# Attention and a maxout expert layer on one core: the probabilities of query blocks 0 and 1 transposed together, and a new order around them

## The chip, the core and the metric

The kernel runs on one NeuronCore of a Trainium2 chip. The metric is the device time of one execution in microseconds (us). The core has five engines with an instruction queue each: TensorE (PE in the profile; its weight loads are shown as PEld), VectorE (DVE), ScalarE (ACT), GpSimd (POOL) and SyncE (SP). SP computes nothing here: it issues nearly all DMAs. Each engine runs its own queue in order and waits on semaphores for the others. TensorE's clock is granted at one of two levels, 1.2 or 2.4 GHz; the profile shows it as a share, 0.50 or 1.00.

## What is computed

```python
# q, k, v: (8, 8, 576, 64) float32; s: (8, 8, 576) float32
scores = q @ k.T / sqrt(64)                        # per batch and head
cum  = cumsum(maximum(s, 0), axis=-1)
bias = -(cum[..., :, None] - cum[..., None, :])
scores = where(causal, -1e9, scores + minimum(bias, 0))
attn = softmax(scores) @ v                         # (8, 8, 576, 64)
x = attn as (4608, 512)                            # heads side by side
h = maximum(maximum(x @ w1, x @ w2), x @ w3)       # (4608, 768)
out = h @ w_out                                    # (4608, 512)
```

## The kernel before

A *visit* is one pair of heads of one batch item. Its 576 queries are five blocks of 128 (the last has 64), and one *step* is one query block of one visit. There are 160 steps and 40 visits. For batch items 0 and 1 a visit is cut in two: blocks 0 and 1 in visits 0 to 7, blocks 2, 3 and 4 in visits 8 to 15. Visits 16 to 39 (items 2 to 7) are *stacked* and have all five blocks. Visits 0 to 3 run in plain float32 and transpose on TensorE; all others keep each number as a sum of two float16 halves, high and low.

In a step, TensorE makes the scores (`scores`, two steps ahead), VectorE their row maximum (`highest`), ScalarE the exponentials (`expo`), and then `probs` divides: ScalarE writes the high halves (tile `prh`), VectorE the low halves (`prl`). SP transposes both by DMA into `ph` and `pl`. One step after the last block of a phase (phase 0: blocks 0 and 1; phase 1: blocks 2 to 4) `values` multiplies the transposed probabilities by `vh` and `vl`, the halves of v, into the PSUM tile `av`. So `values` of blocks 0 and 1 stands at the end of the step after block 1, and that of blocks 2 to 4 at the end of the next visit's block 0. `prh` and `prl` have two buffers each, taken in turn; `ph` and `pl` have one per phase.

When the four visits of an item and phase are done, `add_set` queues 22 expert groups: 18 of 12 matmuls (`pm`, with `x` and the weights `w`) and 4 of 18 (`po`, with `hh` and `hl`). They fill TensorE between the attention's own matmuls. The table `GROUPS` says for each step how many of them run ahead of the next scores and how many at the end of the step. What is left, 43 groups, runs after the last visit.

Loads and preparations stand in lists by step (`at`); the table `moved` shifts single ones by whole steps. For stacked visits these are `load_nat` (a load of 576 KB into `fixed`), the scaling and splitting of q and k (`nat_hi`, `nat_lo`, `nat_own` on GpSimd), and `nat_far`: four DMA copies on SP into the score operands `h` and `l`. `pair_scale2` and `bias_power` put the small matmuls `gmq` and `gmc` on TensorE. `hold` places dummy matmuls on `identb` (table `KEEP`).

In `probs`, for blocks 0 to 3, two transposes leave SP in each step:

```python
for c in range(2):
    nc.sync.dma_start_transpose(
        out=pT[c][:, 0:2 * m, i:i + P], in_=halves[c][:, 0:2 * m, :].rearrange("p n c -> p (n c)")
    )
```

Here m is the number of key blocks (block index + 1), and each has two heads, so block 0 transposes 2 tiles of 128 x 128 for each half, block 1 four, block 2 six and block 3 eight. Block 4 has four issues.

Of the kernel before, what the change touches and what calls it, by code (L numbers as in the profile page):

```python
# [21 lines left out]
"moved": ({('later_keys',): 1, ('load', 10): 1, ('load', 15): 1, ('load', 4): -3, ('load', 5): -3, ('load', 6): -5, ('load', 7):  # L22
-5, ('load_v', 10): 1, ('load_v', 11): -1, ('load_v', 19): -1, ('load_v', 20): 1, ('load_v', 21): 1, ('load_v', 24):
1, ('load_v', 25): 1, ('load_v', 26): 1, ('load_v', 28): 1, ('load_v', 29): 1, ('load_v', 30): 1, ('load_v', 32): 1,
('load_v', 33): 1, ('load_v', 34): 1, ('load_v', 37): 1, ('load_v', 4): -1, ('load_v', 5): -2, ('load_v', 6): -1,
('load_v', 7): -1, ('nat_bias', 18, 1): -1, ('nat_bias', 22, 0): 1, ('nat_bias', 23, 0): -1, ('nat_bias', 26, 0): 1,
('nat_bias', 27, 0): -1, ('nat_bias', 30, 0): 1, ('nat_bias', 34, 0): 2, ('nat_bias', 35, 0): -1, ('nat_bias', 38, 0):
1, ('nat_bias', 39, 0): -1, ('nat_hi', 16, 0): -1, ('nat_hi', 21, 0): -1, ('nat_hi', 21, 1): 1, ('nat_hi', 22, 0): -1,
('nat_hi', 25, 0): -1, ('nat_hi', 26, 0): -1, ('nat_hi', 26, 1): 1, ('nat_hi', 30, 0): -1, ('nat_hi', 30, 1): 1,
('nat_hi', 34, 0): -1, ('nat_hi', 34, 1): 1, ('nat_hi', 37, 0): -1, ('nat_hi', 38, 0): -1, ('nat_hi', 38, 1): 1,  # L30
('nat_own', 21, 0, 0): 2, ('nat_own', 21, 0, 1): 1, ('nat_own', 21, 1, 0): 1, ('nat_own', 21, 1, 1): 1, ('nat_own',
22, 0, 0): 1, ('nat_own', 22, 0, 1): 1, ('nat_own', 22, 1, 0): 1, ('nat_own', 22, 1, 1): 1, ('nat_own', 25, 0, 0): 1,
('nat_own', 25, 0, 1): 1, ('nat_own', 25, 1, 0): 2, ('nat_own', 25, 1, 1): 1, ('nat_own', 26, 0, 0): 1, ('nat_own',
26, 0, 1): 1, ('nat_own', 26, 1, 0): 2, ('nat_own', 26, 1, 1): 1, ('nat_own', 29, 0, 0): 1, ('nat_own', 29, 0, 1): 1,
('nat_own', 29, 1, 0): 1, ('nat_own', 29, 1, 1): 2, ('nat_own', 30, 0, 0): 1, ('nat_own', 30, 0, 1): 1, ('nat_own',
30, 1, 0): 1, ('nat_own', 30, 1, 1): 1, ('nat_own', 33, 0, 0): 1, ('nat_own', 33, 0, 1): 1, ('nat_own', 33, 1, 0): 1,
('nat_own', 33, 1, 1): 1, ('nat_own', 34, 0, 0): 2, ('nat_own', 34, 0, 1): 1, ('nat_own', 34, 1, 0): 1, ('nat_own',
34, 1, 1): 1, ('nat_own', 37, 0, 0): 1, ('nat_own', 37, 0, 1): 1, ('nat_own', 37, 1, 0): 1, ('nat_own', 37, 1, 1): 1,
('nat_own', 38, 0, 0): 1, ('nat_own', 38, 0, 1): 1, ('nat_own', 38, 1, 0): 1, ('nat_own', 38, 1, 1): 1, ('pair_max',
20, 0): 1, ('pair_max', 20, 1): 1, ('pair_max', 21, 0): 1, ('pair_max', 22, 1): 2, ('pair_max', 23, 0): 1,  # L40
('pair_max', 23, 1): 1, ('pair_max', 24, 0): 1, ('pair_max', 24, 1): 1, ('pair_max', 25, 0): 1, ('pair_max', 26, 0):
1, ('pair_max', 26, 1): 1, ('pair_max', 27, 0): 2, ('pair_max', 28, 0): 1, ('pair_max', 28, 1): 1, ('pair_max', 29,
0): 2, ('pair_max', 29, 1): 1, ('pair_max', 30, 0): 1, ('pair_max', 30, 1): 3, ('pair_max', 31, 0): 2, ('pair_max',
31, 1): 1, ('pair_max', 32, 0): 1, ('pair_max', 33, 0): 1, ('pair_max', 33, 1): 1, ('pair_max', 34, 0): 1,
('pair_max', 34, 1): 2, ('pair_max', 35, 0): 2, ('pair_max', 35, 1): 1, ('pair_max', 36, 0): 1, ('pair_max', 36, 1):
1, ('pair_max', 37, 0): 1, ('pair_max', 37, 1): 1, ('pair_max', 38, 0): 1, ('pair_max', 38, 1): 2, ('pair_max', 39,
0): 2, ('pair_max', 39, 1): 1, ('pair_scale3', 3): 1, ('prep2', 10): 1, ('prep2', 9): -1, ('prep3', 5): -1, ('prep3',
7): 1, ('prep3', 8): -1, ('prep5', 11): 1, ('prep5', 15): -1, ('prep5', 17): -1, ('prep5', 18): -1, ('prep5', 4): -1,
('prep5', 5): 1, ('prep5', 7): -1, ('vmax', 17): 1, ('vmax', 20): 1, ('vmax', 21): 2, ('vmax', 22): 1, ('vmax', 24):
1, ('vmax', 25): 1, ('vmax', 26): 1, ('vmax', 28): 1, ('vmax', 29): 1, ('vmax', 30): 1, ('vmax', 32): 1, ('vmax', 33):  # L50
2, ('vmax', 34): 1, ('vmax', 36): 1, ('vmax', 37): 1, ('vmax', 38): 1, ('nat_bias', 36, 1): -1, ('load_nat', 34): 1,
('decode4', 10): 1, ('prep5', 35): -1, ('prep3', 15): 2, ('nat_own', 32, 1, 0): 1, ('nat_far', 29, 0, 1): -1,
('nat_far', 38, 0, 0): 1, ('prep5', 6): -1, ('load_nat', 25): -2, ('nat_own', 24, 1, 1): 1, ('nat_bias', 37, 1): -1,
('nat_far', 23, 1, 1): -1, ('nat_far', 39, 0, 1): 1, ('nat_far', 25, 0, 1): -1, ('nat_own', 39, 0, 1): 1, ('nat_far',
36, 0, 0): -1, ('nat_far', 24, 0, 1): -1, ('nat_far', 18, 1, 0): 1, ('load_nat', 31): 1, ('prep4', 11): 1,
('load_nat', 26): -1, ('nat_far', 38, 1, 0): 1, ('load_nat', 28): -1, ('prep2', 6): 1, ('nat_hi', 24, 0): 1,
('nat_own', 36, 1, 0): 1, ('load_nat', 21): -1, ('prep2', 0): -1, ('decode4', 21): 1, ('nat_bias', 36, 0): -1,
('decode3', 3): -1, ('pair_max', 18, 1): 1, ('gram1', 0, 2): 1, ('prep4', 22): -1, ('decode3', 17): -1, ('load_nat',
27): 1, ('prep5', 13): 1, ('nat_bias', 25, 1): 1, ('load_w', 22): 1, ('nat_far', 28, 0, 0): 1, ('prep2', 3): 1,
('prep2', 11): 1, ('vmax', 39): 1, ('nat_own', 20, 0, 1): 1, ('nat_bias', 22, 1): 1, ('load_v', 31): 1, ('load_nat',  # L60
36): -1, ('nat_bias', 35, 1): -1, ('nat_own', 19, 1, 0): 1}),
# [1449 lines left out]
```

## Time and profile before

| what | value |
|---|---|
| median of 3 runs | 856.54 us (855.1 to 862.59) |
| profiled execution, its own time | 858.63 us |
| its span in the profile | 856.80 us |
| TensorE busy | 810.3 us, 95% |
| VectorE busy | 642.8 us, 75% |
| ScalarE busy | 533.6 us, 62% |
| GpSimd busy | 295.6 us, 35% |
| DMA queue of SP | 237,792 packets, 117 MB |

The busy times overlap, since the engines run side by side. The span is what the profile sees; the execution's own time is 1.83 us longer. Waits are named by the engine that ended them.

### The profile page before, as it was taken

How to read it: one execution, taken by the hardware profiler on the slowest of the kernel's cores; microseconds unless marked ns; L12 is line 12 of the kernel's file. 1: busy time of each engine (PE TensorE's matmuls, PEld its weight loads, DVE VectorE, ACT ScalarE, POOL GpSimd, SP SyncE). 2: the span in 40 equal slices, each digit the busy share in tenths (PEclk: the TensorE clock that was granted, in tenths of full speed). 3: DMA queues.
4: the chain of work that ended last, by engine and by line, in shares of the span. 5: the costliest groups of instructions: out<-in, count | busy, mean ns of one | idle time of the engine just before them, and what ended most of it. 6: DMA issues, size and time to landing. Idle time of an engine off the chain costs nothing.

```text
...
## 1 busy us (share of the span) xinstructions
PE 810.3 (95%) x6933; PEld 618.6 (72%) x6933; DVE 642.8 (75%) x1562; ACT 533.6 (62%) x1458; POOL 295.6 (35%) x532
## 2 busy tenths in 40 slices
...
GB/s 350 369 87 82 123 165 156 189 165 141 142 149 152 118 180 146 146 139 153 145 157 162 134 146 136 155 148 135 179 155 127 125 114 122 99 77 70 17 10 31
DMA packets 238464, 119.81 MB, mean 140 GB/s; under 512 B 210592, under 2 KB 219296, under 8 KB 238368
## 3 DMA queue, kind: packets, MB, share of 16 engines
q1 hardware_dynamic: 237792, 117.01, 63.1%
q10 hardware_dynamic: 576, 1.57, 0.6%
...
## 4 chain that ended last, share of the span: by engine, by line
PE 65%; DVE 16%; DMA 10%; ACT 5%; issue 3%; SPq 1%; POOL 1%; DVEq 0%; ACTq 0%
PE pm L1089 37%; PE po L1131 13%; PE av L957 6%; PE s L631 4%; DVE prl L812 3%; DMA pl<-prl 3%; DMA r<-in_w_dram 2%; DMA ph<-prh 2%; DVE w L1062 2%; DMA st<-in_start_dram 2%; ACT e L766 1%; DVE fixed L228 1%; DVE m L1106 1%; PE s L643 1%; ACT prh L809 1%
## 5 line engine op out<-in xcount | busy, mean ns | idle before, releaser
L1089 PE MATMUL pm<-x,w 128*128 128x320 f16 (+1 forms) x3240 | 424.4, 287 | 1.7 <-DVE m L1106 1.7
L1089 PEld LDWEIGHTS <-w 128*128 128x128 f16 x3240 | 311.8, 98 | 92.6 <-issue 5.8
L1095 POOL CAST hh<-m 128x320 f16<-128x320 f32 (+1 forms) x90 | 45.9, 511 | 348.7 <-DVE m L1106 256.3
L809 ACT ACTIVATE prh<-e,ri 128x128 f16<-128x128 f32 (+3 forms) x200 | 96.8, 529 | 100.5 <-DVE ri L793 90.1
L1106 DVE SCALAR_TENSOR_TENSOR m<-pm,m 128x320 f32<-128x320 f32 (+1 forms) x180 | 81.9, 455 | 91.4 <-PE pm L1089 73.8
L1131 PE MATMUL po<-hh,w 128*128 128x320 f16 (+1 forms) x720 | 141.5, 287 | 1.2 <-ACT kh L333 0.5
L812 DVE SCALAR_TENSOR_TENSOR prl<-e,ri,prh 128x128 f16<-128x128 f32 (+3 forms) x200 | 117.3, 624 | 21.6 <-ACT prh L809 12.8
L1131 PEld LDWEIGHTS <-w 128*128 128x128 f16 x1080 | 103.6, 98 | 33.0 <-issue 4.8
L735 DVE CUSTOM_DVE_ANT_0 s<-s,later,qf 128x128 f32<-128x128 f32 (+1 forms) x192 | 103.8, 551 | 16.8 <-PE s L631 13.7
L766 ACT ACTIVATE e<-s,nm 128x128 f32<-128x128 f32 (+4 forms) x216 | 105.5, 496 | 4.3 <-DVE nm L735 2.0
L1131 PE MATMUL po<-hl,w 128*128 128x320 f16 (+1 forms) x360 | 103.2, 287 | 1.3 <-POOL hl L1096 1.3
L253 POOL COPY h<-fixed 64x576 f16<-64x576 f16 x96 | 72.7, 779 | 56.2 <-DVE fixed L228 54.4
L1103 ACT ACTIVATE m<-pm 128x320 f32<-128x320 f32 (+1 forms) x90 | 36.5, 405 | 74.0 <-PE pm L1089 67.6
L809 ACT ACTIVATE prh<-s,ri 128x512 f16<-128x512 f32 x72 | 46.8, 684 | 41.6 <-DVE ri L793 36.2
L1096 POOL TENSOR_TENSOR hl<-m,hh 128x320 f16<-128x320 f32 (+1 forms) x90 | 69.9, 777 | 7.4
L957 PEld LDWEIGHTS <-vh 128*64 128x64 f16 x800 | 45.8, 110 | 30.1 <-issue 20.9
L1139 ACT ACTIVATE o<-po,os 128x320 f32<-128x320 f32 (+1 forms) x60 | 30.0, 499 | 49.5 <-PE po L1131 43.8
L812 DVE SCALAR_TENSOR_TENSOR prl<-s,ri,prh 128x512 f16<-128x512 f32 x72 | 51.8, 747 | 11.0 <-ACT prl L809 9.9
L957 PE MATMUL av<-ph,vh 128*64 128x320 f16 (+3 forms) x368 | 49.1, 282 | 7.5 <-DMA ph<-prh 7.5
L766 ACT ACTIVATE s<-s,nm 128x512 f32<-128x512 f32 (+1 forms) x72 | 48.5, 673 | 0.1
L631 PE MATMUL s<-h 128*128 128x128 f16 (+1 forms) x192 | 42.3, 299 | 3.4 <-DMA h<-fixed 2.2
L957 PE MATMUL av<-ph,vl 128*64 128x320 f16 (+3 forms) x368 | 44.0, 276 | 0.1
...
## 6 DMA issues: line engine op xcount, KB each, us to landing
...
```

What stands on the lines that cost most here:

```text
L253: nc.gpsimd.tensor_copy(out=R[v]["h"][own, j, x], in_=staged(v)[own, 3 - x])
L631: nc.tensor.matmul(ps[:, j, :nk], lhsT=w[:, c, qs], rhs=w[:, 1 - c, 0:nk], start=(x == "h" and not (lone and j)), stop=(x == "l"), skip_gr ...
L735: nc.vector.tensor_tensor_reduce(out=sc[:, j], in0=sc[:, j], in1=future[0][:, Q4 - nk:Q4], scale=n, scalar=3.0e38, op0=ALU.add, op1=ALU.mi ...
L766: nc.scalar.activation(out=to, in_=sc, func=AF.Exp, bias=nm[:, j:j + 1], scale=-1.0 if below(t) else 1.0, accum_out=sm[:, j:j + 1],)
L809: nc.scalar.activation(out=hi, in_=src, func=AF.Copy, scale=sc)
L812: nc.vector.scalar_tensor_tensor(out=lo, in0=src, scalar=sc, in1=hi, op0=ALU.mult, op1=ALU.subtract)
L957: nc.tensor.matmul(av[j * D:(j + 1) * D, c0:nq], lhsT=lt, rhs=rt, start=(n < 2), stop=(n >= len(todo) - 2), skip_group_check=True,)
L1089: nc.tensor.matmul(pm[:, :nq], lhsT=w[:, wt, kt, :], rhs=xt, start=(n == 0), stop=(n == 3 * NKT - 1))
L1095: nc.gpsimd.tensor_copy(out=st["hh"][:, ft, :nq], in_=m1[:, :nq])
L1096: nc.gpsimd.tensor_tensor(out=st["hl"][:, ft, :nq], in0=m1[:, :nq], in1=st["hh"][:, ft, :nq], op=ALU.subtract)
L1106: nc.vector.scalar_tensor_tensor(out=m1[:, :nq], in0=pm[:, :nq], scalar=HSC, in1=m1[:, :nq], op0=ALU.mult, op1=ALU.max)
L1131: nc.tensor.matmul(pm[:, :nq], lhsT=W[18 + ft][:, wt, dt, :], rhs=st[ht][:, ft, :nq], start=(n == 0), stop=(n == 3 * NFT - 1),)
```

## The change

For blocks 0 and 1 on the float16 path (28 visits: 4 to 7 and 16 to 39), block 0 takes a pair of tiles `prh`, `prl` and writes its two 128 x 128 pieces into places 0 and 1, and issues nothing. Block 1 takes the same pair, writes its four pieces into places 2 to 5, and one issue for each half transposes all six. The transposed tile is [128, 6, 128] instead of [128, 4, 256], and `values` reads the columns of key block 0 from two places of it, in a pattern of two runs of 128. The numbers of matmuls and their columns stay.

```diff
         ph = 0 if qb < 2 else 1
         if qb in (0, 2):
             PT[v, ph] = [
-                att.tile([P, 4 + (4 + 2 * n) * ph, PH[ph][1]], F16, tag=f"pT{c}{ph}", name=f"p{c}{t}", bufs=1)
+                att.tile([P, 4 + (4 + 2 * n) * ph, PH[ph][1]] if ph else [P, 6, P], F16, tag=f"pT{c}{ph}", name=f"p{c}{t}", bufs=1)
...
-        halves = [att.tile([P, 8, P], F16, tag=f"pr{c}", name=f"pr{c}{t}") for c in "hl"]
+        if qb == 1:
+            halves = PR.pop(t - 1)
+        else:
+            halves = [att.tile([P, 8, P], F16, tag=f"pr{c}", name=f"pr{c}{t}") for c in "hl"]
+        if qb == 0:
+            PR[t] = halves
         if nj == 2:
             m = qb + 1
             i = (qb - 2 * ph) * P
-            hv, lv = (x[:, 0:2 * m, :].rearrange("p (m j) c -> p m j c", j=2) for x in halves)
+            o = 2 if qb == 1 else 0
+            hv, lv = (x[:, o:o + 2 * m, :].rearrange("p (m j) c -> p m j c", j=2) for x in halves)
...
-        if nj == 2:
+        if qb == 1:
+            for c in range(2):
+                nc.sync.dma_start_transpose(
+                    out=pT[c][:, 0:6, :], in_=halves[c][:, 0:6, :].rearrange("p n c -> p (n c)")
+                )
+        elif nj == 2 and ph:
...
-                        todo.append((j, r[vt][:, j, kb, :], pT[t][:, 2 * kb + j, c0:nq], c0))
+                        rt = pT[t][:, 2 * kb + j, c0:nq] if ph else pT[t][:, j + 4 * kb:j + 3 + 2 * kb:2, :]
+                        todo.append((j, r[vt][:, j, kb, :], rt, c0))
...
-"KEEP": ({('a', 69): 4}),
+"KEEP": ({('b', 37): 2, ('d', 69): 10, ('b', 70): 18}),
```

The tables `moved`, `fetched` and `GROUPS` have new numbers as well. Preparations, copies and loads shift by one step, now and then by two; the groups move by one or two places and number 309 before the tail in both kernels. Two places on SP's queue show what this makes of it. In the rows below, `prh55` is the high half written in step 55, `ph55` the transposed tile; `fixed` is the target of `load_nat`, `rv` a load of v.

SP around steps 55 and 56, which are blocks 0 and 1 of visit 19, before:

```order
L815 DMA_TRANSPOSE ph55_4281<-prh55_4285 128x2x128
L815 DMA_TRANSPOSE pl55_4282<-prl55_4286 128x2x128
L1140 DMA out_dram<-o1_1_2_4295 128x320
L196 DMA rv23_4311<-in_qkv_dram 128x640
L217 DMA fixed3_2061<-in_pair_dram 128x1152
L815 DMA_TRANSPOSE ph55_4281<-prh56_4349 128x4x128
L815 DMA_TRANSPOSE pl55_4282<-prl56_4350 128x4x128
L1140 DMA out_dram<-o1_1_3_4393 128x320
L257 DMA h20_4235<-fixed5_2693 64x1152
```

And now (a merged tile keeps the name of its block 0):

```order
L1167 DMA out_dram<-o1_1_0_4188 128x320
L230 DMA fixed3_2030<-in_pair_dram 128x1152
L209 DMA rv23_4240<-in_qkv_dram 128x640
L1167 DMA out_dram<-o1_1_1_4266 128x320
L835 DMA_TRANSPOSE ph55_4216<-prh55_4220 128x6x128
L835 DMA_TRANSPOSE pl55_4217<-prl55_4221 128x6x128
L1167 DMA out_dram<-o1_1_2_4326 128x320
L270 DMA h20_4210<-fixed5_2678 64x1152
```

The first pair is gone, and the pair load `fixed3` stands two places further ahead of the transposes that `values` of visit 19 needs.

SP around steps 65 and 66, blocks 0 and 1 of visit 21, up to the copies of visit 22, before:

```order
L815 DMA_TRANSPOSE ph65_4984<-prh65_4988 128x2x128
L815 DMA_TRANSPOSE pl65_4985<-prl65_4989 128x2x128
L1140 DMA out_dram<-o2_0_0_5031 128x256
L815 DMA_TRANSPOSE ph65_4984<-prh66_5074 128x4x128
L815 DMA_TRANSPOSE pl65_4985<-prl66_5075 128x4x128
L1140 DMA out_dram<-o2_0_1_5119 128x256
L196 DMA rv25_5122<-in_qkv_dram 128x640
L257 DMA h22_5039<-fixed5_2693 64x1152
L257 DMA l16_2765<-fixed5_2693 64x1152
```

And now:

```order
L1167 DMA out_dram<-o2_0_0_4986 128x256
L1167 DMA out_dram<-o2_0_1_5020 128x256
L835 DMA_TRANSPOSE ph65_4974<-prh65_4978 128x6x128
L835 DMA_TRANSPOSE pl65_4975<-prl65_4979 128x6x128
L209 DMA rv25_5086<-in_qkv_dram 128x640
L270 DMA h22_4950<-fixed5_2678 64x1152
L270 DMA l16_2749<-fixed5_2678 64x1152
```

The copies into `h` and `l` stand at the same place behind block 1, with two transposes fewer ahead of them.

## Rows read from the trace of the kernel before

**Rows 1.** The page: an engine's busy time, share of the span, instructions.

```profile
PE 810.3 (95%) x6933; PEld 618.6 (72%) x6933; DVE 642.8 (75%) x1562; ACT 533.6 (62%) x1458; POOL 295.6 (35%) x532
```

**Rows 2.** By stretch: length, PE, PEld, DVE, ACT, POOL, PEclk, DMA share, GB/s.

```profile
0.00:120.00 120.00, 99.29 (x643) 81.03 (x644) 102.08 (x229) 89.99 (x244) 11.98 (x34) 0.97 0.59 193
120.00:240.00 120.00, 113.14 (x1007) 85.94 (x1006) 99.60 (x196) 80.58 (x206) 64.62 (x110) 1.00 0.81 165
240.00:440.00 200.00, 185.97 (x1650) 138.68 (x1648) 163.55 (x427) 131.43 (x371) 76.01 (x134) 0.99 0.73 147
440.00:780.00 340.00, 338.51 (x3031) 254.90 (x3029) 266.09 (x689) 221.77 (x618) 128.67 (x230) 1.00 0.68 134
```

**Rows 3.** Waits of TensorE, 120 to 440 us: total, times, longest.

```profile
PE av L957 <- DMA ph<-prh: 5.7, 4, 3.5
PE av L957 <- DMA pl<-prl: 2.7, 5, 1.0
PE s L631 <- DMA h<-fixed: 2.2, 2, 1.2
PE gmq L506 <- DVE ri L793: 2.1, 1, 2.1
PE gmc L506 <- DVE m L1106: 1.9, 1, 1.9
...
PE s L631 <- DMA l<-fixed: 1.2, 2, 0.8
```

**Rows 4.** Tile `ph`: issues of transposes on SP, duration ns minimum/median/maximum.

```profile
L815 SPq DMA_TRANSPOSE ph<-prh x120: 1167/1232/3458, 50.4 to 772.4; - x120
```

**Rows 5.** Timeline of SP, steps 55 and 56: start, us, what it issues.

```profile
296.80 1.18 SPq L815 DMA_TRANSPOSE ph<-prh  x1
298.08 2.40 SPq L815 DMA_TRANSPOSE pl<-prl  x1
...
301.63 0.45 SPq L217 DMA_DIRECT2D fixed<-in_pair_dram  x1
302.17 1.19 SPq L815 DMA_TRANSPOSE ph<-prh  x1
```

**Rows 6.** Timeline of ScalarE: the high half of step 56.

```profile
298.99 0.91 ACT L809 ACTIVATE prh<-e,ri 128x256 f16<-128x256 f32 x2 [0.32 <-DVE ri L793]
```

**Rows 7.** Timeline of TensorE at `values` of visit 19, blocks 0 and 1.

```profile
306.83 0.43 PE L957 MATMUL av<-ph,vh 128*64 128x256 f16 x2 [3.54 <-DMA ph<-prh]
```

**Rows 8.** DMA issues, us to landing: at 302 us; quiet, six tiles; quiet, four.

```profile
ph<-prh SPq DMA_TRANSPOSE x1, 4.6
...
ph<-prh SPq DMA_TRANSPOSE x1, 2.8
...
ph<-prh SPq DMA_TRANSPOSE x1, 2.5
```

**Rows 9.** Busy time as in rows 2, behind the stall of rows 7.

```profile
306.80:310.20 3.40, 3.37 (x23) 2.40 (x24) 1.74 (x3) 2.48 (x6) 0.00 (x0) 0.50 1.00 240
```

**Rows 10.** Timeline of TensorE: the first scores of visit 22.

```profile
356.29 0.22 PE L631 MATMUL s<-h 128*128 128x128 f16 x1 [1.07 <-DMA h<-fixed]
```

**Rows 11.** Timeline of TensorE: gram of raw weights, one element in four read.

```profile
50.80 1.00 PE L1017 MATMUL av<-r 128*128 128x128 bf16 x7
```

**Rows 12.** Timeline of TensorE: the dummy matmuls of step 69 and what follows.

```profile
360.24 0.39 PE L885 MATMUL av<-identb 128*128 128x128 bf16 x4
360.46 0.38 PE L631 MATMUL s<-h 128*128 128x256 f16 x2
```

**Rows 13.** Timeline of TensorE: `values` of blocks 0 and 1 without a wait.

```profile
610.35 0.30 PE L957 MATMUL av<-ph,vh 128*64 128x256 f16 x2
...
610.97 0.50 PE L1089 MATMUL pm<-x,w 128*128 128x256 f16 x3
```

**Rows 14.** Waits of ScalarE and VectorE for landings, 120 to 440 us.

```profile
ACT prh L809 <- DMA ph<-prh: 8.3, 5, 2.8
...
DVE prl L812 <- DMA pl<-prl: 6.3, 5, 2.4
```

More of the change, by code (lines that the diff above doesn't have):

```diff
@@ L21 @@
 PLAN = {
[L22 to L41, printed above, removed]
@@ L57 @@
[L57 to L61, printed above, removed]
+"moved": ({('later_keys',): 1, ('load', 10): 2, ('load', 4): -2, ('load', 5): -3, ('load', 6): -5, ('load', 7): -5, ('load_v',
@@ new lines @@
+11): -1, ('load_v', 19): -1, ('load_v', 20): 1, ('load_v', 24): 1, ('load_v', 25): 1, ('load_v', 28): 1, ('load_v',
+29): 1, ('load_v', 30): 1, ('load_v', 32): 1, ('load_v', 34): 2, ('load_v', 37): 1, ('load_v', 4): -1, ('load_v', 5):
+-1, ('load_v', 6): -1, ('load_v', 7): -1, ('nat_bias', 18, 1): -1, ('nat_bias', 23, 0): -1, ('nat_bias', 30, 0): 1,
+('nat_bias', 34, 0): 2, ('nat_bias', 38, 0): 2, ('nat_hi', 21, 1): 1, ('nat_hi', 22, 0): -1, ('nat_hi', 25, 0): -1,
+('nat_hi', 26, 0): -1, ('nat_hi', 26, 1): 1, ('nat_hi', 30, 0): -1, ('nat_hi', 30, 1): 1, ('nat_hi', 34, 0): -1,
@@ new lines @@
+('nat_own', 30, 1, 1): 2, ('nat_own', 33, 0, 0): 1, ('nat_own', 33, 0, 1): 1, ('nat_own', 33, 1, 0): 1, ('nat_own',
+33, 1, 1): 1, ('nat_own', 34, 0, 0): 1, ('nat_own', 34, 0, 1): 1, ('nat_own', 34, 1, 0): 2, ('nat_own', 34, 1, 1): 2,
+('nat_own', 37, 0, 1): 1, ('nat_own', 37, 1, 1): 1, ('nat_own', 38, 0, 0): 1, ('nat_own', 38, 0, 1): 1, ('nat_own',
+38, 1, 0): 1, ('nat_own', 38, 1, 1): 1, ('pair_max', 20, 0): 2, ('pair_max', 21, 0): 1, ('pair_max', 22, 1): 2,
+('pair_max', 23, 0): 2, ('pair_max', 23, 1): 1, ('pair_max', 24, 0): 1, ('pair_max', 24, 1): 1, ('pair_max', 25, 0):
@@ new lines @@
+1, ('pair_max', 26, 0): 1, ('pair_max', 26, 1): 1, ('pair_max', 27, 0): 2, ('pair_max', 28, 0): 1, ('pair_max', 28,
+1): 1, ('pair_max', 29, 0): 2, ('pair_max', 30, 0): 1, ('pair_max', 30, 1): 3, ('pair_max', 31, 0): 1, ('pair_max',
+31, 1): 1, ('pair_max', 32, 0): 1, ('pair_max', 33, 0): 1, ('pair_max', 33, 1): 1, ('pair_max', 34, 0): 2,
+('pair_max', 34, 1): 2, ('pair_max', 35, 0): 2, ('pair_max', 36, 0): 1, ('pair_max', 36, 1): 1, ('pair_max', 37, 1):
+1, ('pair_max', 38, 0): 2, ('pair_max', 38, 1): 2, ('pair_max', 39, 0): 2, ('pair_max', 39, 1): 1, ('pair_scale3', 3):
@@ new lines @@
+1, ('prep2', 10): 1, ('prep2', 9): -1, ('prep3', 5): -1, ('prep3', 7): 1, ('prep3', 8): -1, ('prep5', 11): 1,
+('prep5', 15): -1, ('prep5', 17): -1, ('prep5', 18): -1, ('prep5', 4): -1, ('prep5', 7): -1, ('vmax', 17): 1, ('vmax',
+20): 1, ('vmax', 21): 2, ('vmax', 22): 2, ('vmax', 24): 1, ('vmax', 25): 1, ('vmax', 26): 1, ('vmax', 28): 1, ('vmax',
+30): 2, ('vmax', 32): 1, ('vmax', 33): 1, ('vmax', 34): 2, ('vmax', 36): 1, ('vmax', 37): 2, ('load_nat', 34): 1,
+('decode4', 10): 1, ('prep3', 15): 2, ('nat_far', 29, 0, 1): -1, ('nat_far', 38, 0, 0): 1, ('load_nat', 25): -1,
@@ new lines @@
+('nat_own', 24, 1, 1): 1, ('nat_bias', 37, 1): -1, ('nat_far', 23, 1, 1): -1, ('nat_own', 39, 0, 1): 1, ('nat_far',
+24, 0, 1): -1, ('nat_far', 18, 1, 0): 1, ('load_nat', 31): 1, ('load_nat', 26): -2, ('nat_far', 38, 1, 0): 1,
+('load_nat', 28): -1, ('nat_hi', 24, 0): 1, ('nat_own', 36, 1, 0): 1, ('load_nat', 21): -1, ('prep2', 0): -1,
+('decode4', 21): 2, ('nat_bias', 36, 0): -1, ('pair_max', 18, 1): 1, ('prep4', 22): -1, ('decode3', 17): -1,
+('load_nat', 27): 1, ('prep5', 13): 1, ('nat_bias', 25, 1): 2, ('nat_far', 28, 0, 0): 1, ('prep2', 3): 1, ('prep2',
@@ new lines @@
+11): 1, ('vmax', 39): 1, ('nat_own', 20, 0, 1): 1, ('nat_bias', 22, 1): 1, ('load_v', 31): 1, ('load_nat', 36): -1,
+('nat_bias', 35, 1): -2, ('nat_far', 35, 1, 1): 1, ('nat_bias', 38, 1): 1, ('nat_bias', 29, 1): 1, ('nat_hi', 17, 0):
+-1, ('prep4', 24): -1, ('prep5', 14): -1, ('nat_hi', 16, 0): -1, ('prep5', 38): 1, ('nat_far', 32, 1, 1): 1,
+('nat_own', 31, 0, 1): 1, ('pair_scale1', 2): -1, ('nat_hi', 28, 0): 1, ('nat_far', 32, 1, 0): -1, ('nat_bias', 30,
+1): 1, ('nat_far', 35, 0, 0): -1, ('nat_far', 36, 1, 1): 1, ('bias4', 0): 1, ('nat_far', 21, 1, 1): 1, ('decode4',
@@ new lines @@
+22): 1, ('load_v', 35): -1, ('prep4', 35): -2, ('vmax', 18): 1, ('load_w', 10): -1, ('nat_hi', 35, 0): 1, ('load_w',
+7): 1, ('nat_hi', 27, 0): -1, ('nat_bias', 24, 0): 1, ('prep3', 6): -1, ('prep5', 24): -1, ('pair_scale3', 4): 1,
+('load_nat', 35): -1, ('load_nat', 39): 1, ('nat_own', 35, 1, 0): 2, ('nat_hi', 33, 0): 1, ('nat_bias', 23, 1): 1,
+('nat_far', 31, 1, 1): -1, ('prep4', 23): 1, ('nat_far', 29, 1, 0): -1, ('nat_own', 28, 1, 1): 1, ('prep4', 15): -1,
+('load_v', 22): -1, ('load_nat', 32): 1, ('load_v', 10): 1, ('nat_far', 35, 1, 0): -1, ('sign', 2): 1, ('sign', 15):
@@ new lines @@
+1, ('nat_bias', 26, 1): -1, ('nat_far', 21, 0, 1): 1, ('nat_bias', 28, 1): -1, ('nat_own', 23, 1, 1): 2, ('prep4',
+27): -1, ('load_w', 5): -1, ('nat_far', 28, 1, 0): 1, ('prep4', 9): 1, ('nat_far', 34, 0, 1): -1, ('pair_max', 16, 1):
+-1, ('nat_far', 17, 1, 1): -1, ('prep3', 14): 1, ('prep4', 10): 1, ('nat_bias', 17, 1): -1, ('load_w', 8): -1,
+('nat_own', 32, 1, 1): 1, ('nat_own', 31, 1, 1): 1, ('prep2', 15): -1, ('pair_max', 25, 1): 1, ('nat_far', 32, 0, 0):
+1, ('prep4', 33): -2, ('prep3', 4): 1, ('decode3', 12): -1, ('prep4', 28): -1, ('prep4', 26): 1, ('nat_hi', 32, 0): 1,
@@ new lines @@
+('nat_hi', 18, 1): -1, ('decode1', 20): -1, ('nat_hi', 31, 0): -1, ('nat_own', 27, 0, 1): 1, ('prep4', 38): 1,
+('load_nat', 24): -1, ('nat_far', 34, 0, 0): 1, ('nat_bias', 28, 0): -1, ('vmax', 19): -1, ('prep5', 19): -1,
+('pair_max', 17, 0): 1, ('prep4', 29): -1, ('nat_far', 24, 1, 0): -1, ('prep4', 34): -2, ('nat_far', 36, 0, 1): 1,
+('vmax', 6): 1, ('nat_bias', 25, 0): -1, ('vmax', 29): 1, ('nat_lo', 38, 1): 1, ('nat_own', 23, 0, 1): 1, ('nat_lo',
+29, 0): -1, ('load_nat', 33): -1, ('decode1', 2): -1, ('nat_bias', 31, 1): 1, ('nat_own', 19, 1, 1): 1, ('load_nat',
```

32 lines of the change are left out of this document (13 added, 19 removed), and 20 rows, old and new, of the table PLAN.

## The prediction

> **What bounds the kernel now.** I read the busy times of the page first, then busy time by stretch, then the waits of the engine that is nearly always busy, and then, place by place, the queue that releases those waits. TensorE is busy 810.3 us, 95% of the span [rows 1]. By stretch [rows 2] it is idle for 120 - 99.3 = 20.7 us before 120 us, 120 - 113.1 = 6.9 us from 120 to 240, 200 - 186.0 = 14.0 us from 240 to 440, and 1.5 us from 440 to 780. After 440 us nothing but work for TensorE counts, and the change takes none of it away: both group tables run 309 of the 352 expert groups up to the end of the attention, and the last 43 follow in the tail. So the most that it can bring back after the start-up is the 20.9 us of idle time between 120 and 440.
>
> The waits of TensorE in that stretch [rows 3] are mostly for landings: `ph` 5.7 us, `pl` 2.7, and the score operands `h` 2.2 and `l` 1.2, together 11.8 us of 20.9. All of them come through SP. One transpose holds that queue for 1.232 us in the middle [rows 4], whatever its size, and there are 368. The queue runs in order, so a late one delays all behind it. The longest stall shows how: the high half of step 56 is written by 298.99 + 0.91 = 299.90 us [rows 6], but SP is then in the transposes of step 55 (1.18 and 2.40 us), an output, a value load and a pair load of 576 KB; it comes to step 56 at 302.17 [rows 5]. That transpose lands 4.6 us later, behind the load [rows 8], and TensorE stands still for 3.54 us [rows 7].
>
> **The change, part by part.** The sum is made against the profiled execution: 858.63 us, of which the span is 856.80. It lies 2.1 us above the median of the runs, 856.54, so 2.1 is taken off at the end.
>
> 1. *Fewer issues.* 28 visits have blocks 0 and 1 on this path (4 early, 24 stacked). Each loses two transposes: 56 x 1.232 = 69 us of SP's time. None of it is TensorE's; it counts only where SP is late and TensorE waits.
> (a) The 3.54 us stall, `values` of visit 19. Without the pair of step 55, 3.6 us of SP, the pair load is issued by 302.1 - 3.6 = 298.5, and the merged issue can go 302.17 - 299.90 = 2.3 us sooner. Landing costs 2.8 us for six blocks in an empty queue and 4.6 behind a load [rows 8], so 302.7 to 304.5 against TensorE's arrival at 306.83 - 3.54 = 303.3: 0 to 1.2 us of stall is left, 2.3 to 3.5 gone. I take -3.0.
> (b) The four copies of `h` and `l` stand behind both pairs of the visit; at visit 22 TensorE waits 1.07 us for them [rows 10]. Two issues fewer bring them 2.5 us forward, more than any wait for them (the longest is 1.2 [rows 3]). The one at the first stacked visit has no pair ahead of it. Of 3.4 us I take -2.2 (bounds -1.0 and -3.4).
> (c) The rest of `ph` and `pl`, 5.7 + 2.7 - 3.5 = 4.9 us, is for blocks 2 to 4. Their eight transposes keep their own issue times, so only lateness inherited from the steps before goes. I take -3.0 (bounds 0 and -4.9).
> 2. *Clock.* Behind the 3.54 us stall the granted clock is 0.50, the lower level, for 3.4 us [rows 9]: 1.7 us lost. A stall of at most 1.2 us should not bring it: -1.3 (bounds 0 and -1.7).
> 3. *Six blocks at once.* The last transpose before `values` now carries six blocks, not four: 2.8 us to land against 2.5 [rows 8]. That counts only where TensorE already waited for this half, which of the 28 visits are 5 and 19: +0.5 (bounds 0 and +1).
> The Trainium skill ("DMA: Bandwidth & Descriptors", section "Latency and other measured facts") gives 261 GB/s for a transpose with a non-contiguous middle dimension against some 350 to 400 for a contiguous one; the tile of blocks 0 and 1 becomes contiguous. By that the six blocks would land about as soon as four did, and this term would be 0. No row here has a contiguous one.
> 4. *The strided operand.* `values` now reads the same columns as two runs of 128. The nearest row with a strided moving operand is the gram of the raw weights, one element in four: 1.00 us for 7, so 0.14 us each [rows 11], against 0.055 for the contiguous `identb` matmuls, 4 in 0.22 us [rows 12]. The block of 12 takes 610.97 - 610.35 = 0.62 us [rows 13]; 28 of them at 0.14 / 0.055 = 2.6 times that are +28 us at the far end. Runs of 128 elements are much nearer to the contiguous row, so I take 0.
> 5. *Dummy matmuls.* 30 instead of 4, 28 of them between the scores of steps 71 and 72: 26 x 0.055 = +1.4 us, or nothing if TensorE waits there anyway. +0.5.
> 6. *Reordering.* The two longest waits of 120 to 440 that are not landings, for the powers `gmq` 2.1 and `gmc` 1.9 us [rows 3], are waits for VectorE; the matmuls ahead of `gmc` stand in the same order in both kernels. Small moves elsewhere: -1.0 (bounds -4 and +3). In the start, decodes and loads move by a step at most while VectorE is busy 102 of 120 us [rows 2]: 0 (bounds -2 and +2).
> 7. *What is late next.* Where TensorE no longer waits for a landing it meets ScalarE or VectorE, which are in the same loop: the wait for `gmq` at 280 us grows when the one at 272 us goes. +1.5 (bounds 0 and +3). It is no more than that because these two wait for the same queue: ScalarE 8.3 and VectorE 6.3 us for a probability tile still being transposed [rows 14]. Blocks 0 and 1 now share one such tile, four in rotation per visit instead of five.
>
> Sum: -3.0 - 2.2 - 3.0 - 1.3 + 0.5 + 0 + 0.5 - 1.0 + 0 + 1.5 = -8.0, so 850.6 for an execution like the profiled one and **848.5** for the median, 0.9% below 856.5. The bounds of 1 to 3 and 7 put it between 844 and 853.
>
> **The rivals.** *The queue was not the cost* (0.24): SP had room, the late transposes were late because ScalarE and VectorE wrote them late, and a TensorE freed of one landing waits for the next engine. For it: VectorE is busy 163.6 of 200 us from 240 to 440 [rows 2], and the two longest waits that are not for landings are for it [rows 3]. Against it: the 2.3 us between tile written and transpose begun. Left would be parts of (a) and (b), some -2.5, and +1 for the dummies: 855.
> The Trainium skill has a rule of this kind ("DMA: Bandwidth & Descriptors", section "Issuing engines are not separate DMA queues"): the sequencer's time to start a DMA is usually small beside the DMA itself. By that rule alone, 56 issues fewer would bring nothing, some 856. The trace disagrees for transposes: 1.232 us of issue [rows 4] beside 2.5 to 2.8 us to landing [rows 8].
>
> *The whole loop closes* (0.19): with SP free, ScalarE and VectorE run ahead as well, and the new order fits them. Three quarters of the 20.9 us and of the 1.7 us of clock return: -16.5, so 840. Against it: the waits for VectorE among the 20.9 have no reason to go.
>
> *The merged pair lands late* (0.12): slower. All of blocks 0 and 1 now leaves SP in one step, behind whatever load stands there, and `values` comes one step later. In the old kernel half of it was gone a step before. Where a load stands ahead, landing took 4.6 us and SP itself was held 2.40 us in one issue [rows 5, 8]. If the merged pair lands 3 us later than the old second pair did, those visits wait in which the low half had landed less than 3 us before its use, by the trace 6 of the 28 (5, 18, 19, 21, 24 and 29): 3 + 1 + 3 + 1 + 3 + 0 = 11 us, and two of the 3 us stalls bring a 1.7 us clock loss each; with the 4 us that (b) and part of (c) still give, 856.5 + 11 + 3.4 - 4 = 867. It decides from about 2 us of added lateness on; below 1 us it is term 3. What speaks against it is the load that the new order puts further ahead of the pair at visit 19.
>
> **How the numbers follow.** The forecast, 844 to 853, gets 0.45. A difference below 1% (8.6 us) is about what a measurement of this kernel cannot tell from none: the runs shown span 855.1 to 862.6. Faster by over 1% means below 848.0: nearly half of the forecast and all of the closed loop, 0.45 / 2 + 0.19, some 0.42. Slower by over 1% is above 865.1: the late pair, 0.12. The rest, 0.46, lies within 1%. The range runs from 838, just below the closed loop, to 858, just above the idle queue; it leaves out the late pair and the ends of the others, under 2 in 10. The far end of term 4 lies outside it, with little chance.
>
> **What would show it.** 312 transposes at an unchanged 1.2 us each; TensorE's waits for `ph`, `pl`, `h` and `l` between 120 and 440 us down from 11.8 us to about 4; no stretch at the lower clock near 300 us; TensorE's busy time up by the dummies alone, so the 12 matmuls of `values` for blocks 0 and 1 still in 0.6 us; waits for VectorE up by a microsecond or two. I am wrong if these waits shrink and the time does not (something else is late), or if `ph` waits now stand at `values` of blocks 0 and 1.

## The result, and the profile after

The changed kernel takes 850.46 us (median of 8 runs, 848.67 to 852.99), the kernel before 859.56 us beside it (8 runs, 855.1 to 863.21). The ratio is 0.9882, with a 95% interval of 0.9854 to 0.9909: 10.1 us faster by the ratio, where 8.0 were forecast. The profiled execution took 851.2 us, its span is 849.40 us. The figure came out; whether the reasons did is the matter of the experiments.

The page's busy line, for [rows 1]:

```profile
PE 812.0 (96%) x6959; PEld 622.6 (73%) x6959; DVE 639.0 (75%) x1562; ACT 533.8 (63%) x1458; POOL 296.6 (35%) x532
```

TensorE is busy 1.7 us longer. The 26 dummy matmuls more, at 0.055 us each, would make 1.4 of that, but a second profile of the changed kernel (from its run in *The start*, below) has 814.1 us, so the difference is no larger than that between two executions. Busy time by stretch, with the columns of [rows 2]:

```profile
0.00:120.00 120.00, 97.98 (x608) 79.07 (x610) 99.54 (x222) 86.99 (x239) 9.89 (x32) 0.93 0.57 184
120.00:240.00 120.00, 114.88 (x1008) 87.61 (x1005) 99.96 (x195) 80.27 (x205) 66.28 (x108) 0.99 0.79 169
240.00:440.00 200.00, 193.67 (x1760) 146.42 (x1759) 169.66 (x443) 138.03 (x386) 77.94 (x142) 1.00 0.79 156
440.00:780.00 340.00, 339.47 (x3060) 257.56 (x3061) 259.65 (x682) 219.94 (x612) 128.31 (x226) 1.00 0.66 133
```

TensorE's idle time in the four stretches is now 22.0, 5.1, 6.3 and 0.5 us; it was 20.7, 6.9, 14.0 and 1.5 [rows 2]. Nearly all that came back, 7.7 us, lies between 240 and 440. The second profile has 21.4, 4.3, 4.9 and 0.3 us. TensorE's waits from 120 to 440 us, for [rows 3]:

```profile
PE av L983 <- DMA ph<-prh: 2.6, 3, 1.5
PE av L983 <- DMA pl<-prl: 1.8, 3, 0.8
PE gmc L519 <- DVE m L1133: 1.6, 1, 1.6
PE s L644 <- DMA h<-fixed: 1.5, 1, 1.5
...
PE s L644 <- DMA l<-fixed: 0.3, 1, 0.3
```

The same in the second profile, where the wait of 1.5 us for `h` is put down to GpSimd:

```profile
PE av L983 <- DMA ph<-prh: 1.3, 2, 1.0
PE av L983 <- DMA pl<-prl: 1.2, 2, 0.9
...
PE s L644 <- DMA l<-fixed: 0.5, 2, 0.3
```

The waits for landings fell from 11.8 to 6.2 us, and to 3.0 in the second profile (4.5 with that one); the wait for `gmq` (2.1 us in [rows 3]) has no row any more in either. There are 312 transposes, and the merged ones hold SP no longer than those of [rows 4]; tile `ph`, high halves of blocks 0 and 1:

```profile
L835 SPq DMA_TRANSPOSE ph<-prh x28: 1210/1217/2174, 58.7 to 753.8; - x28
```

The timeline of SP at visit 19, for [rows 5]:

```profile
297.29 0.42 SPq L230 DMA_DIRECT2D fixed<-in_pair_dram  x1
...
299.92 1.23 SPq L835 DMA_TRANSPOSE ph<-prh  x1
```

The DMA issues of that moment, us to landing, for [rows 8]; then the line of all merged issues:

```profile
ph<-prh SPq DMA_TRANSPOSE x1, 5.1
```
```profile
DMA to landing us min/median/max: 2.7/2.8/5.7
```

The timeline of TensorE at that `values`, for [rows 7], and at `values` of blocks 0 and 1 without a wait, for [rows 13]:

```profile
305.09 0.30 PE L983 MATMUL av<-ph,vh 128*64 128x256 f16 x2 [0.79 <-DMA ph<-prh]
...
603.57 0.30 PE L983 MATMUL av<-ph,vh 128*64 128x256 f16 x2
...
604.19 1.48 PE L1116 MATMUL pm<-x,w 128*128 128x256 f16 x12
```

SP takes the merged half up as soon as it is written, 2.25 us sooner than before, and the stall shrinks from 3.54 to 0.79 us. The 12 matmuls take 604.19 - 603.57 = 0.62 us, as before: the strided operand costs nothing. The granted clock is 1.00 behind this `values` now (it was 0.50 in [rows 9]), but the start has more at 0.50:

```profile
52.20:59.00 6.80, 5.84 (x22) 4.56 (x22) 4.14 (x15) 3.74 (x8) 0.22 (x1) 0.50 0.20 82
...
219.50:222.90 3.40, 3.40 (x15) 1.90 (x15) 0.83 (x4) 1.34 (x2) 1.98 (x5) 0.50 1.11 96
```

Another 3.4 us lie at 35 us and 6.8 us at 90 us, so 20.4 us in all at the lower clock, against 10.2 us in the execution before. That is a matter of single executions: the mean granted clock is 0.988 over the eight of the changed kernel, and 0.988 over the 29 of the kernel before that ran with later experiments. Read alone, this profile supports the forecast: the queue of SP was freed, and the waits for landings halved. The experiments say that this is half the story.

### The profile page after: what moved, and what is told of

Same layout as the page of the kernel before. It is cut to its first block, busy times and chain, and to the rows that moved or that the text cites. A ratio compares the mean times of both kernels' runs of the same rounds, so it can differ in the third digit from the quotient of the medians.

```text
span 849.4 us, 19371 instructions
## 1 busy us (share of the span) xinstructions
PE 812.0 (96%) x6959; PEld 622.6 (73%) x6959; DVE 639.0 (75%) x1562; ACT 533.8 (63%) x1458; POOL 296.6 (35%) x532
## 4 chain that ended last, share of the span: by engine, by line
PE 76%; DMA 8%; DVE 8%; ACT 4%; issue 1%; SPq 1%; POOL 1%; ACTq 0%; DVEq 0%; POOLq 0%
PE pm L1116 42%; PE po L1158 14%; PE av L983 6%; PE s L644 5%; PE pm L1187 3%; DMA r<-in_w_dram 2%; DMA pl<-prl 2%; DVE prl L832 2%; DMA st<-in_start_dram 2%; PE s L656 1%; ACT prh L829 1%; PE po L1209 1%; DMA l<-fixed 1%; PE s L699 1%; DMA ph<-prh 1%
## 5 line engine op out<-in xcount | busy, mean ns | idle before, releaser
L832 DVE SCALAR_TENSOR_TENSOR prl<-e,ri,prh 128x128 f16<-128x128 f32 (+3 forms) x200 | 113.2, 604 | 10.9 <-ACT prh L829 5.2
L266 POOL COPY h<-fixed 64x576 f16<-64x576 f16 x96 | 74.6, 792 | 72.1 <-DVE fixed L241 69.9
L241 DVE SCALAR_TENSOR_TENSOR fixed<-fixed,qf,fixed 128x576 f16<-128x576 f32 x48 | 40.9, 886 | 4.4 <-ACT fixed L237 4.4
```

The lines of the kernel that those rows point to most:

```text
L266: nc.gpsimd.tensor_copy(out=R[v]["h"][own, j, x], in_=staged(v)[own, 3 - x])
L832: nc.vector.scalar_tensor_tensor(out=lo, in0=src, scalar=sc, in1=hi, op0=ALU.mult, op1=ALU.subtract)
```

## Experiments

All ratios are to the kernel before, run beside the kernel on the same chip.

### The merge alone and the tables alone

The change has two halves: the merged transposes, and new numbers in `moved`, `fetched`, `GROUPS` and `KEEP`. Each was put alone. The merge with the old tables:

```diff
 # the changed kernel
-PLAN = {"moved": new, "fetched": new, "GROUPS": new, "KEEP": {('b', 37): 2, ('d', 69): 10, ('b', 70): 18}, ...}
+PLAN = {"moved": old, "fetched": old, "GROUPS": old, "KEEP": {('a', 69): 4}, ...}
```

> The merged transposes with the old tables (groups, moved steps, fetches, 4 dummy matmuls). Theory (the freed queue of SP gives the gain): the waits for ph, pl, h and l from 120 to 440 us fall from 11.8 us to about 6, the end of step 24 stays where it was before (the changed kernel is 4.3 us later there), and the time is 11 us below the kernel before or a little less: 846 to 851 us. Rival (the new tables give the gain, the merge only makes room for them): 857 to 861 us, and the waits for landings stay near 10 us.

Measured: 859.18 us (12 runs), ratio 0.9995, interval 0.9968 to 1.0022. The theory fell and the rival's figures came: the merge alone brings nothing that can be told from none. And the old code with the new tables:

```diff
 # the kernel before
-PLAN = {"moved": old, "fetched": old, "GROUPS": old, "KEEP": {('a', 69): 4}, ...}
+PLAN = {"moved": new, "fetched": new, "GROUPS": new, "KEEP": {('b', 37): 2, ('d', 69): 10, ('b', 70): 18}, ...}
```

> The old separate transposes, 368 of them, with the new tables. Theory (the freed queue gives the gain): the 4 us that the changed kernel loses by step 24 are lost here too and nothing comes back, 861 to 866 us, with at least 11 us of waits for landings from 120 to 440 us. Rival (the tables give the gain): 850 to 853 us.

Measured: 853.91 us (12 runs), ratio 0.9934 (0.9903 to 0.9965). Neither side's figure: the tables bring about 5.7 us by themselves, and the merge another 4.5 on top of them (0.9934 to 0.9882), though nothing without them. By the intervals of the two ratios these 4.5 us are known to be between some 1 and 8.

Why the merge brought nothing in the old order can be seen in its trace. TensorE's waits from 120 to 440 us, merge with old tables:

```profile
PE av L983 <- DMA pl<-prl: 4.9, 5, 2.1
PE s L644 <- DMA h<-fixed: 3.1, 4, 1.5
...
PE av L983 <- DMA ph<-prh: 2.0, 2, 1.4
...
PE gmq L519 <- DVE ri L807: 1.8, 1, 1.8
```

`ph` fell from 5.7 to 2.0 us, as forecast, but `pl` rose from 2.7 to 4.9 and `h` from 2.2 to 3.1: the waits for landings are 10.0 us together, against 11.8. Those for other engines hardly changed, 8.7 us against 9.0. TensorE in the same trace, at visit 19 and at `values` of blocks 2 to 4 of visit 24:

```profile
305.15 0.30 PE L983 MATMUL av<-ph,vh 128*64 128x256 f16 x2 [1.36 <-DMA ph<-prh]
307.92 0.27 PE L1116 MATMUL pm<-x,w 128*128 128x256 f16 x1 [0.70 <-ACT x L993]
308.84 1.69 PE L1116 MATMUL pm<-x,w 128*128 128x256 f16 x14 [0.65 <-DVE x L994]
...
435.68 0.65 PE L983 MATMUL av<-pl,vh 128*64 128x320 f16 x8 [2.14 <-DMA pl<-prl]
```

The stall of 3.54 us shrinks to 1.36. But the next expert groups read the `x` that this very `values` makes, and wait 0.70 and 0.65 us for it (0.65 under the new tables as well); at visit 24 a wait of 2.14 us for `pl` stands where 0.92 for `ph` and 0.35 for `pl` were. The last transpose of that `pl` left SP sooner than before, at 431.73 us and not at 433.07, but took longer to land. Its row of DMA issues, before and with the merge alone:

```profile
pl<-prl SPq DMA_TRANSPOSE x1, 2.4
...
pl<-prl SPq DMA_TRANSPOSE x1, 3.9
```

Nor do the copies for visit 22 come forward by two issues. SP before, then VectorE and SP with the merge alone:

```profile
351.06 0.47 SPq L257 DMA_DIRECT2D h<-fixed  x1
...
345.87 1.70 DVE L832 SCALAR_TENSOR_TENSOR prl<-e,ri,prh 128x256 f16<-128x256 f32 x2
...
347.63 1.21 SPq L835 DMA_TRANSPOSE pl<-prl  x1
...
350.03 0.47 SPq L270 DMA_DIRECT2D h<-fixed  x1
```

The copies stand behind the merged transposes on SP, and these wait until VectorE has written the low half of block 1, at 347.57; so the copies leave 1.0 us sooner, not 2.5, and TensorE waits 1.10 us for them where it waited 1.07. TensorE is idle 14.1 us from 240 to 440, against 14.0 before [rows 2], and 5.1 from 120 to 240, against 6.9. The clock did no better: the stretch at 0.50 near 306 us is gone, and another stands at 281:

```profile
281.00:284.40 3.40, 3.40 (x22) 1.82 (x19) 3.40 (x9) 2.60 (x7) 0.00 (x0) 0.50 1.19 196
```

With the new tables and separate transposes the landing waits are not shorter than that, but those for VectorE are. The same stretch, tables alone:

```profile
PE av L957 <- DMA ph<-prh: 4.3, 4, 1.4
PE av L957 <- DMA pl<-prl: 3.2, 5, 1.0
PE s L631 <- DMA l<-fixed: 2.2, 5, 0.7
```

Landings take 10.5 us (with 0.8 for `h`); there is no wait for `gmq`, none of `pm` for `m`. Idle time from 240 to 440 is 10.5 us. Merge and tables together have 6.3.

### The issues put back

Is it SP's time that the merge gives under the new tables, or the merged landing, or the shared tiles? In the changed kernel block 0 now also transposes its two pieces for nothing:

```diff
+        if qb == 0:
+            for c in range(2):
+                nc.sync.dma_start_transpose(
+                    out=att.tile([P, 2, P], F16, tag=f"dead{c}", name=f"dead{c}{t}", bufs=1),
+                    in_=halves[c][:, 0:2, :].rearrange("p n c -> p (n c)")
+                )
         if qb == 1:
```

> The changed kernel with the 56 issues put back on SP as dead ones: at block 0 of each of the 28 visits both halves of that block are also transposed into a tile that nothing reads; the merged transposes stay. Theory (what the merge brings under the new tables, 853.9 - 850.5 = 3.4 us, is SP's time): it goes back to the time of the new tables with separate transposes, 853 to 855 us, with the waits for landings from 120 to 440 us back at 10 us. Rival (it comes from the later single use, the shared tiles or the landing of six blocks at once): 850 to 851.5 us.

Measured: 854.39 us (12 runs), ratio 0.9939 (0.9914 to 0.9964), the same as with separate transposes. SP at visit 19, then TensorE:

```profile
294.88 1.18 SPq L835 DMA_TRANSPOSE dead<-prh  x1
296.16 1.18 SPq L835 DMA_TRANSPOSE dead<-prl  x1
...
299.81 1.24 SPq L841 DMA_TRANSPOSE ph<-prh  x1
```
```profile
302.81 0.30 PE L989 MATMUL av<-ph,vh 128*64 128x256 f16 x2 [1.44 <-DMA ph<-prh]
```

The waits for landings come to 8.8 us (6.2 and 3.0 without the dead issues, 10 were expected). So under the new tables what the merge is worth goes when SP's time goes, and no part of it is seen to come from the merged landing or the shared tiles. A dead transpose also moves two tiles. That was not tried apart, but the traces show no cost of it: merged transposes land in 2.8 us at the median with and without the dead ones, those of blocks 2 and 3 in 3.3 with and 3.4 without, and those of block 4 in 2.4 either way.

### More issues in the old order

If 56 issues fewer brought nothing in the old order, do 56 more cost nothing? The kernel before, with the same six lines of dead transposes ahead of its own:

> The kernel before, old tables and separate transposes, with 56 dead transposes more (block 0 of each of the 28 visits, into a tile that nothing reads): 424 issues instead of 368. Theory (in the old order the waits for other engines stand next to those for SP, so SP's time is worth little there): as 312 issues brought nothing, 424 cost little, 859 to 862 us. Rival (the old order sits at the edge of what SP can do, so fewer issues bring nothing but more cost as much as under the new tables, 4 us or more): 863 to 868 us.

Measured: 898.88 us (6 runs), ratio 1.0442 (1.0412 to 1.0471), 38 us slower, where the rival expected 4 to 9. Three timelines of SP show one visit each, from the first issue of block 4 to the next visit's. The kernel before:

```profile
614.60 2.46 SPq L821 DMA_TRANSPOSE ph<-prh  x2
617.17 3.58 SPq L821 DMA_TRANSPOSE pl<-prl  x2
620.86 1.18 SPq L815 DMA_TRANSPOSE ph<-prh  x1
...
638.33 1.17 SPq L821 DMA_TRANSPOSE ph<-prh  x1
```

The merge alone:

```profile
614.73 2.46 SPq L846 DMA_TRANSPOSE ph<-prh  x2
617.30 2.49 SPq L846 DMA_TRANSPOSE pl<-prl  x2
622.95 1.21 SPq L835 DMA_TRANSPOSE ph<-prh  x1
...
638.34 1.17 SPq L846 DMA_TRANSPOSE ph<-prh  x1
```

And with 56 more:

```profile
621.78 3.56 SPq L827 DMA_TRANSPOSE ph<-prh  x2
...
629.36 1.17 SPq L815 DMA_TRANSPOSE dead<-prh  x1
...
647.98 1.17 SPq L827 DMA_TRANSPOSE ph<-prh  x1
```

Before, SP is without a pause for this whole round of 23.7 us but for some 0.1 us between issues, and still the round is no longer than with the merge (23.6), where SP stands idle from 619.79 to 622.95. With 56 more it is 26.2. Over all 24 stacked visits (first issue of block 4 of the first and of the last one, divided by 23) a round is 23.18 us before, 23.17 with the merge, 24.93 with more issues; 23 x 1.75 = 40 us. SP's pauses longer than 0.3 us, summed over the same rounds, are 1.3 us a round before, 4.5 with the merge and 0.6 with more issues. So the old kernel stood near the corner. TensorE's work sets the round there (busy 338.5 of 340 us after 440 [rows 2]), with SP just able to follow: 2.4 us less for SP per round bring nothing, 2.4 us more cost 1.75, and TensorE has room, as its stretch with 56 more shows:

```profile
440.00:780.00 340.00, 322.36 (x2865) 243.44 (x2865) 259.08 (x669) 212.21 (x590) 126.29 (x230) 0.99 0.66 136
```

Here, too, the data of the dead transposes are not seen to cost anything: the others land as before, in 3.2 us at the median for blocks 0 to 3 and 2.4 for block 4.

### Which table

Merged transposes and the old start (up to step 24) throughout; behind it only part of the new tables. First the groups (the expectation names the fetches too, but all five that differ stand ahead of step 24, so none changes here):

```diff
-PLAN = {"moved": old, "fetched": old, "GROUPS": old, ...}
+PLAN = {"moved": old, "fetched": old, "GROUPS": old[:24] + new[24:], ...}
```

> Merged transposes, the old tables up to step 24, and behind it of the new tables only the expert groups and the fetches of their weights; the moved preparations, copies and loads and the 4 dummies are the old ones. With all new tables behind step 24 it was 847.1, with none 859.2. Theory (the gain is that other expert groups stand where TensorE waited): 847 to 851 us. Rival (the gain is that preparations and loads are moved): 856 to 860 us.

Measured: 855.26 us (12 runs), ratio 0.9957 (0.9935 to 0.9978). Then only the moved steps:

```diff
-PLAN = {"moved": old, "fetched": old, "GROUPS": old, ...}
+PLAN = {"moved": new behind 24, "fetched": old, "GROUPS": old, ...}
```

> Merged transposes, the old tables up to step 24, and behind it of the new tables only the moved preparations, copies and loads; groups, fetches and the 4 dummies are the old ones. Theory (the groups give the gain): 856 to 860 us. Rival (the moves give it): 847 to 851 us. If both this one and the one with new groups alone stay above 853, only the two together bring it.

Measured: 857.04 us (12 runs), ratio 0.9968 (0.9944 to 0.9991). Against the merge alone (0.9995) the groups give some 3.3 us, the moves 2.3, which by itself is inside the two intervals; both together behind step 24 (with the new dummies) gave 12 and 9.5 us in two sets of runs (below). Neither came to the 847 to 851 us that one table alone should have brought, and both stay above 853, the sign that was named for the two being needed together.

### The start

By the profile, the changed kernel ends step 24 at 139.3 us and the kernel before at 135.0. So the changed kernel got the old start:

```diff
-PLAN = {"moved": new, "fetched": new, "GROUPS": new, ...}
+PLAN = {"moved": old up to 24, then new, "fetched": old, "GROUPS": old[:24] + new[24:], ...}
```

> The changed kernel with the old tables for everything that stands ahead of step 24 in both (groups, moved steps and fetches). Theory (the new tables cost 4 us in the first 135 us, and nothing behind makes them good): step 24 ends about 4 us sooner than in the changed kernel and the time is 845 to 848 us. Rival (what is lost there is taken in by idle time behind it): 849 to 852 us, with longer waits between 120 and 440 us.

Measured: 847.11 us (6 runs), ratio 0.9861 (0.9825 to 0.9897). This looked like a version that beats both, so it ran again beside the changed kernel.

> The same kernel as the one with the old start, again, beside the changed kernel on one chip: 847.1 us as in its first run, 3 to 4 us below the changed kernel, if the old start is better; within 1 us of it if that was chance.

> The changed kernel again, for the comparison on one chip: 850.5 us as in its first runs.

Measured: 850.35 us for the old start, ratio 0.9889 (0.9862 to 0.9916), and 849.69 us for the changed kernel, ratio 0.9876 (0.9850 to 0.9901), 6 runs each. The gain did not come again. In both profiles of the old start step 24 ends at 135 us, and both executions have 10.2 us at the lower clock; each was the fastest of its six. The other ten take up to 5 us longer. Nine of them have a lower mean clock, but one has a higher (0.996) and took 848.3 us, so the clock is not all of it. A difference of 3 us between medians of six runs is not to be trusted here.

### The dummies

```diff
-"KEEP": ({('b', 37): 2, ('d', 69): 10, ('b', 70): 18}),
+"KEEP": ({}),
```

> The changed kernel without its 30 dummy matmuls, whose result nothing reads. By the prediction's term 5: 0.5 us faster than the changed kernel, 1.4 at most, 849 to 850 us. Rival (they keep the granted clock up through a wait behind step 69): a stretch at the lower clock appears near there and the time is 1 to 2 us longer, 851 to 853 us.

Measured: 849.59 us, ratio 0.9890 (0.9852 to 0.9928). With the old start as well:

> Merged transposes, old tables up to step 24, new ones behind it, and none of the 30 dummy matmuls. If the old start and the missing dummies add up: 847.1 - 0.9 = 846.2 us. If the dummies do something for the wait behind step 69 that the old start uncovers: 847 to 849 us.

Measured: 851.42 us, ratio 0.9884 (0.9851 to 0.9918). Neither differs from the changed kernel by more than the runs spread.

### The low half of block 4 from another queue

The waits that are left at `values` of blocks 2 to 4 are for the last of four transposes in a row. Two of them were given to ScalarE:

```diff
-                    nc.sync.dma_start_transpose(
+                    (nc.scalar if c else nc.sync).dma_start_transpose(
                         out=pT[c][:, 0:8 + 2 * c, 256:320]...
```

> Merged transposes, old start, new tables behind step 24 (847.1 us), and the two transposes of the low half of block 4 of each visit issued by ScalarE in place of SP. The waits that are left at the values of blocks 2 to 4 are for the last of these, which leaves SP 3 to 6 us after its data are written. Theory (SP's queue of four issues in a row is what they wait for): these waits, 2.5 us in all, go and the time is 844 to 846 us. Rival (ScalarE now stands in its own queue until VectorE has written the low half, and its exponentials come late): 849 to 856 us, with new waits of VectorE and TensorE for ScalarE.

Measured: 1071.89 us, ratio 1.2463 (1.2415 to 1.2511). The rival was right in direction, but far too mild, and what ScalarE waits for is not what it named. The timelines of SP and of ScalarE at one visit (VectorE has written its low half by 606.87):

```profile
605.72 3.28 SPq L846 DMA_TRANSPOSE ph<-prh  x2
```
```profile
610.28 2.70 ACTq L846 DMA_TRANSPOSE pl<-prl  x2
613.08 0.44 ACT L1130 ACTIVATE m<-pm 128x320 f32<-128x320 f32 x1 [7.19 <-issue]
```

SP's second `ph` was issued at 607.75 and landed 2.4 us later, at 610.14; ScalarE began at 610.28. It had been in a semaphore wait until 610.16, which that landing ended. In all 32 visits its transposes stand behind such a wait and begin 0.07 to 0.23 us after the last one on SP has landed. Meanwhile its exponentials and its part of the expert groups stand behind them. The mean granted clock of this execution is 0.909, so part of the loss is TensorE at the lower level between its waits. The Trainium skill ("DMA: Bandwidth & Descriptors", section "Silent corruption: two transposing streams in flight at once") has this as a rule: transposes from a second engine have to wait until those of the first are complete. The program as built carries the wait, and the trace shows what it costs.

## Why the prediction was right in the figure and wrong in its reasons

1. *Fewer issues*, -8.2 us as (a) to (c): this is the step that failed. The merge alone, in the order for which the term was worked out, holds terms 1 to 4 and 7, -7.5 us together, and measured -0.4 us (0.9995; bounds -2.7 and +1.9). By its trace (a) gave 2.2 us, the stall of 3.54 us fell to 1.36, but 1.35 us of waits for `x` came behind it; (b) gave 0.3 (3.4 to 3.1), since the copies wait in SP's queue behind transposes that wait for their data; and (c) lost 0.6 (4.9 to 5.5), since a transpose that left sooner did not land sooner. The term took idle time that ended last at SP's transfers as idle time that SP's issuing alone had caused. With the new order 56 issues are worth 4.5 us, and it is SP's time, since dead issues take it away again.
2. *Clock*, -1.3: the stretch near 306 us went, but others came, in the merge alone as well as in the changed kernel, and the mean granted clock over the executions is 0.988 before and after. Nothing was gained.
3. *Six blocks at once*, +0.5: not seen apart. The dead issues, with the landing of six kept, gave the time of separate transposes, which bounds it by their intervals, about 3 us. The Trainium skill ("DMA: Bandwidth & Descriptors", section "Latency and other measured facts") has a faster rate for a contiguous transpose, by which this term would be nothing. It is not seen at this size: six contiguous tiles land in 2.7 us at the least and 2.8 at the median, and six with gaps (block 2) in 2.7 at the least, too. The price for landing at visit 19 was too low: 5.1 us, not 2.8 to 4.6, though the load stands two places further ahead.
4. *The strided operand*, 0: right, 0.62 us.
5. *Dummies*, +0.5: within what the runs can tell.
6. *Reordering*, -1.0 (bounds -4 and +3): mis-sized. The tables alone give 5.7 us (3.0 to 8.3), more than the bound of 4 at the middle. What they take away most of are the waits for other engines, 9.0 us before and 4.1 with the tables: the wait for `gmq`, 2.1 us, which 7 expected to grow, and those of `pm` for `m`, 1.7. The remark that the matmuls ahead of `gmc` did not move was right (1.9 before, 1.6 now), but it says nothing of `gmq`. That the start costs 0 is as near as the runs can tell (850.35 us with the old start, 849.69 with the new), though the profile seemed to show 4 us.
7. *What is late next*, +1.5 (at most 3): hardly seen. With the merge the waits for other engines went from 9.0 to 8.7 us in the old order, and from 4.1 to 4.5 in the new one. The two waits for `x` behind visit 19 are of this kind; the wait for `gmq`, which was named, fell to 1.8.

That the sum held is luck, because two errors met: the tables gave 5.7 us where term 6 has 1.0, and all the rest 4.5 where the other terms sum to 7.0. The bounds, too, were narrower than what they were made from: those of 1 to 3 and 7, added up, reach from 842.5 to 856.7, not from 844 to 853. The rival that the queue was not the cost has 1.5 us of gain, and describes the merge alone (0.4 us). Its reason holds in part: at visit 19 a TensorE freed of one landing waits for the next engine, and merged transposes wait for their data. But SP had little room, 1.3 us of pauses in a round of 23.2. The prediction set beside it a rule of the Trainium skill ("DMA: Bandwidth & Descriptors", section "Issuing engines are not separate DMA queues"): the time to start a DMA is usually small beside the DMA. For this queue it does not hold: 424 issues of 1.2 us, which land in 2.4 to 3.2 us at the median, set the pace of the whole kernel. The closed loop and the late pair did not come. The issue of 2.40 us that spoke for the late pair stands ahead of the loads in [rows 5], not behind one.

Of what was to be seen, the 312 transposes, the quiet clock near 300 us and the 0.62 us of `values` came; the busy time did within what two executions differ by; the waits for landings fell to 6.2 us in one profile and to 3.0 or 4.5 in the other, where about 4 were forecast; and waits for VectorE fell where they should have risen.

Still open is why tables and merge together give more than both apart. The excess is some 4 us, and by the intervals of the ratios alone it could be anything from 0 to 8. The traces bear it out as idle time from 240 to 440 us (14.1 with the merge, 10.5 with the tables, 6.3 and 4.9 with both, 14.0 with neither), wait by wait, but no single table carries it.
